# Streaming the weight chunks straight from the input tensors instead of from a contiguous copy in DRAM

## The chip, the cores and the metric

One core of a Trainium2 chip runs the whole kernel. The metric is device time in microseconds (us); medians of several executions are quoted.

## The reference

Two independent parts write the two halves of the output. Part A (a long convolution by Fourier transform) is not touched by the change, except that it shares the DMA engines. Part B is a chain of 64 segments, each a small attention layer that hands 8 memory rows to the next one:

```
for s in range(n_seg):                       # 64 segments of 32 rows
    h = concat(mem, x[32*s : 32*s+32])       # 40 x 1024
    q, k, v = h @ Wq, h @ Wk, h @ Wv         # 1024 x 4096 each
    o = softmax(mask(q k^T * scale)) v       # 32 heads of 128
    o = o @ Wo                               # 4096 x 1024
    mem = o[:8]; out[s] = o[8:]
```

The four matrices are 32 MB in bf16. They do not fit into SBUF, and each segment needs all of them.

## The kernel before

The weights are cut into 64 chunks of 128 x 2048 elements (512 KB, 4 KB per partition). 43 stay in SBUF (`Wearly`, `Wlate`). 21 are streamed; one of these is kept in PSUM, so every segment loads 20: fourteen of the projections (four of Wk, five of Wq, five of Wv) and six of Wo. Loads go to a ring of six tiles, `wring`. A load is issued when the matmuls of an earlier chunk release their ring tile.

```python
W_v = [w.rearrange("(kc p) (g c) -> kc g p c", p=128, g=2) for w in (Wk, Wq, Wv)]
Wo_v = Wo.rearrange("(hp hh e) d -> hp e hh d", hh=2, e=128)
...
def dram_chunk(ch):                 # where the chunk lies in the input tensor
    m, a, g = ch
    return Wo_v[a] if m == 3 else W_v[m][a, g]

def stream_src(ch):                 # where it lies in the copy
    return WS[ring_order.index(ch), :, 0:2048]
...
WS = dram.tile([len(ring_order), 128, PITCH], BF, name="WS")      # PITCH = 2048: contiguous
for ch in ring_order:
    if ch[0] == 3:                  # Wo chunks: DRAM to DRAM, at the start
        nc.gpsimd.dma_start(dst_view(stream_src(ch), ch), dram_chunk(ch))
...
# set-up of part B: the projection chunks pass through SBUF once anyway and are written to WS
nc.sync.dma_start(t[:], dram_chunk(ch))
if ch in streamed:
    nc.gpsimd.dma_start(stream_src(ch), t[:])
...
def fetch():                        # the segment loop
    if loads:
        s, ch = loads.pop(0)
        live[s, ch] = t = ring.tile([128, 2048], BF, tag="wring", name="wring")
        nc.sync.dma_start(t[:], stream_src(ch))
```

So each load reads 512 KB that lie in one piece. In the inputs, a projection chunk is 128 rows of 4 KB that lie 8 KB apart (a row of 4096 elements is shared by two chunks), and a Wo chunk is two runs of 2 KB per partition.

## Time and profile before

| | |
|---|---|
| time | 2419.2 us (2403.4 to 2421.8, 3 runs) |
| set-up (part A, and part B's set-up), until the first `wring` load is issued | 563.8 us |
| segment loop | 1855 us, 28.7 us per segment |

The windows view of the kernel before, over three stretches of the loop; the last columns are the granted TensorE clock, the mean busy share of the 16 DMA engines and the bytes moved per time:

```profile
core 0: us, PE busy (x) PEld busy (x) DVE busy (x) ACT busy (x) POOL busy (x), PEclk, DMA share, GB/s
600.00:1200.00 600.00, 468.98 (x10469) 238.39 (x10468) 164.03 (x615) 142.28 (x273) 87.61 (x294) 0.96 0.99 381
1200.00:1800.00 600.00, 469.17 (x10414) 239.59 (x10418) 163.85 (x614) 141.92 (x272) 87.16 (x293) 0.96 0.98 380
1800.00:2400.00 600.00, 469.26 (x10467) 241.81 (x10460) 164.03 (x614) 142.28 (x273) 86.83 (x292) 0.96 0.98 380
```

The DMA engines are busy 98 to 99% of the time; TensorE is not (469 of 600 us). The chain of waits of the same kernel, by engine and then by line:

```profile
DMA 43%; PE 27%; issue 4%; ACT 1%; DVE 1%; POOL 0%; DVEq 0%; SPq 0%; POOLq 0%; ACTq 0%
DMA wring<-WS 43%; PE acc L708 16%; PE yacc L796 4%; PE tail_acc L657 2%; PE tps L723 1%; PE tps L627 1%; PE S L731 1%; PE S L727 1%; ACT Y L855 1%; PE OTp L769 0%; DVE rec L628 0%; PE S L734 0%; DMA rec<-REC 0%; PE OTp L773 0%; DMA out_dra
```

Waiting for a streamed chunk is the largest part of the chain. The DMA view of the loop (600 to 2400 us): packets of all queues, and the loads with their median time from issue to landing:

```profile
DMA packets 194189, 684.92 MB, mean 381 GB/s; under 512 B 27815, under 2 KB 27815, under 8 KB 193889
...
wring<-WS SPq DMA_DIRECT2D x1255, 512.0 KB, 7.4
```

At 381 GB/s one load of 512 KB takes 1.4 us of the engines, but 7.4 us to land: about five are queued on average. The packet records of the trace show 4096 B packets with a mean of 167 ns.

SyncE's timeline, where the loop's first loads are issued (start, length, instruction):

```profile
563.83 6.58 SPq L597 DMA_DIRECT2D wring<-WS  x6
```

Below is one segment close to the average; the rows are 0–3, 3–8, 8–11, 11–16 and 16–28 us after the segment's start, which here means the ScalarE copy that ends the segment before it (`Y<-yacc`).

```profile
969.59:972.59 3.00, 2.23 (x22) 0.92 (x26) 1.43 (x3) 0.37 (x1) 2.12 (x7) 0.57 1.03 406
972.59:977.59 5.00, 4.84 (x81) 2.05 (x76) 0.42 (x1) 1.17 (x2) 0.00 (x0) 0.92 0.95 308
977.59:980.59 3.00, 1.92 (x32) 0.78 (x28) 0.42 (x1) 0.58 (x1) 0.00 (x0) 1.00 1.00 388
980.59:985.59 5.00, 3.98 (x85) 1.72 (x81) 1.11 (x3) 1.40 (x3) 0.90 (x5) 1.00 1.02 413
985.59:997.59 12.00, 8.78 (x269) 5.06 (x269) 4.31 (x21) 3.51 (x7) 0.57 (x1) 1.00 1.03 406
```

SyncE issues no load for about four us around a segment's start: the tile of a segment's last chunk goes to the chunk that returns from PSUM, so by the code the next load waits until the new segment has used its first streamed chunk (averaged over the segments: the last issue 1.2 us before the start, the next 3.0 us after it). Then six loads follow within 5 us. The rate falls to about 300 GB/s and is back at 413 some ten microseconds later. The engines are also less busy in it: their mean share in the 3–8 us stretch is 0.86 (packet records, 58 segments), though it is 0.98 to 0.99 over the loop.

### The profile page before, as it was taken

The numbers are of one execution on the slowest core, as the hardware profiler recorded it, in microseconds if no ns is written. First come the engines' busy times: TensorE is split into PE (matmuls) and PEld (weight loads), VectorE is DVE, ScalarE is ACT, GpSimd is POOL, SyncE is SP. The second block draws the span as 40 slices with busy tenths as digits, with TensorE's granted clock in tenths as the row PEclk, the third lists the DMA queues.
The fourth block names the chain that finished last, engine by engine and source line by source line (L and its number), as shares of the span: only waits on it lengthen the run. The fifth ranks groups of instructions, "written<-read, shape, count | busy, mean of one in ns | idle before, by whom it ended". The sixth has DMA issues, their size and how long they took to land.

```text
span 2419.0 us, 76567 instructions
## 1 busy us (share of the span) xinstructions
PE 1773.0 (73%) x33620; PEld 883.9 (37%) x33620; DVE 755.4 (31%) x2331; ACT 640.0 (26%) x1143; POOL 365.4 (15%) x1019
## 2 busy tenths in 40 slices
PE   2665369764787777777778778778778777777876
PEld 1221034322343434434343434343434343444433
DVE  5978321111222222222223222222222222222222
ACT  6965011111222222222222222222222222222222
POOL 5034100000111111111111111111111111111111
PEclk9788669887999999999999998999999999999999
DMA  8886974659999999999999999999999999999997
GB/s 290 311 282 206 369 264 114 201 192 389 383 376 396 372 388 378 395 365 375 388 379 399 373 381 370 399 362 379 364 384 384 379 363 382 369 399 375 373 390 284
DMA packets 308487, 842.05 MB, mean 348 GB/s; under 512 B 83676, under 2 KB 91900, under 8 KB 308151
## 3 DMA queue, kind: packets, MB, share of 16 engines
q1 hardware_dynamic: 277992, 767.72, 83.3%
q0 software_dynamic: 20048, 45.76, 5.5%
q10 hardware_dynamic: 10112, 23.68, 2.9%
q8 instruction: 263, 4.31, 0.7%
q14 instruction: 72, 0.59, 0.1%
HBM read 777.66 MB, written 62.39 MB: 347 GB/s over the span
## 4 chain that ended last, share of the span: by engine, by line
DMA 43%; PE 27%; issue 4%; ACT 1%; DVE 1%; POOL 0%; DVEq 0%; SPq 0%; POOLq 0%; ACTq 0%
DMA wring<-WS 43%; PE acc L708 16%; PE yacc L796 4%; PE tail_acc L657 2%; PE tps L723 1%; PE tps L627 1%; PE S L731 1%; PE S L727 1%; ACT Y L855 1%; PE OTp L769 0%; DVE rec L628 0%; PE S L734 0%; DMA rec<-REC 0%; PE OTp L773 0%; DMA out_dram<-Y 0%
## 5 line engine op out<-in xcount | busy, mean ns | idle before, releaser
L708 PEld LDWEIGHTS <-rec 128*32 128x32 bf16 x12288 | 322.2, 98 | 568.2 <-issue 324.5
L708 PE MATMUL acc<-wring,rec 128*32 128x512 bf16 x3840 | 396.6, 396 | 164.0 <-DMA wring<-WS 156.4
L717 ACT CAST qkv_sb<-acc 128x512 bf16<-128x512 f32 x384 | 224.7, 585 | 824.2 <-PE acc L708 824.2
L708 PE MATMUL acc<-Wearly,rec 128*32 128x512 bf16 x4608 | 383.5, 404 | 17.1 <-DVE rec L628 17.0
L708 PE MATMUL acc<-Wlate,rec 128*32 128x512 bf16 x3840 | 332.7, 388 | 0.3 <-issue 0.3
L796 PEld LDWEIGHTS <-OT 128*32 128x32 bf16 x8192 | 221.4, 100 | 259.8 <-issue 191.8
L796 PE MATMUL yacc<-Wlate,OT 128*32 128x256 bf16 x5120 | 239.7, 288 | 41.3 <-issue 41.1
L796 PE MATMUL yacc<-wring,OT 128*32 128x256 bf16 x3072 | 173.8, 288 | 123.3 <-DMA wring<-WS 103.0
L685 POOL COPY KT<-rec 128x128 bf16<-128x128 bf16 x128 | 38.3, 299 | 649.9 <-PE S L734 550.7
L628 DVE COPY rec<-tps 128x64 bf16<-128x64 bf16 x64 | 12.3, 192 | 383.6 <-PE tps L627 378.8
L739 DVE TENSOR_REDUCE mx<-S 128x5 f32<-128x200 f32 x128 | 47.1, 368 | 269.8 <-PE S L734 262.8
L861 POOL DMA_DIRECT2D out_dram<-Y x64 | 45.9, 717 | 517.6 <-ACT Y L855 508.7
L782 ACT CAST OT<-OTp 128x512 bf16<-128x512 f32 x128 | 74.9, 585 | 174.7 <-PE OTp L773 170.1
L855 ACT CAST Y<-yacc 128x256 bf16<-128x256 f32 x64 | 23.8, 372 | 305.1 <-PE yacc L796 305.1
L723 PE MATMUL tps<-ident,qkv_sb 128*128 128x128 bf16 x1024 | 101.9, 222 | 0.0
L621 POOL DMA_DIRECT2D rec<-REC x64 | 37.3, 583 | 405.7 <-issue 199.9
L786 DVE CAST OTB<-OTp 128x128 bf16<-128x128 f32 x128 | 34.7, 271 | 195.1 <-ACT OT L782 195.1
L815 DVE COPY KT<-tps 128x512 bf16<-128x512 bf16 x64 | 27.2, 425 | 216.5 <-PE tps L723 216.5
L723 PEld LDWEIGHTS <-qkv_sb 128*128 128x128 bf16 x1024 | 58.1, 98 | 82.2 <-issue 65.9
L540 PE MATMUL kb_ps<-XBT,Wearly 128*128 128x512 bf16 x288 | 84.2, 383 | 1.2 <-ACT XBT L507 1.2
L692 POOL COPY QBm<-rec 128x32 bf16<-128x32 bf16 x512 | 83.8, 209 | 0.0
L818 DVE COPY QT<-tps 128x512 bf16<-128x512 bf16 x64 | 27.2, 425 | 165.0 <-PE tps L723 165.0
(201 smaller groups left out, 2256.7 us busy)
## 6 DMA issues: line engine op xcount, KB each, us to landing
wring<-WS SPq DMA_DIRECT2D x1281, 512.0 KB, 7.4
rec<-REC POOLq DMA_DIRECT2D x64, 192.0 KB, 6.3
SK<-s_sb SPq DMA_DIRECT2D x16, 512.0 KB, 4.5
SU<-s_sb SPq DMA_DIRECT2D x16, 512.0 KB, 3.9
Kg<-SK ACTq DMA_DIRECT2D x32, 256.0 KB, 4.7
Ug<-SU SPq DMA_DIRECT2D x32, 256.0 KB, 5.3
REC<-stage SPq DMA_DIRECT2D x4, 2048.0 KB, 13.2
pw<-in_B_Wv_dram SPq DMA_DIRECT2D x16, 512.0 KB, 8.4
```

Source lines behind the costliest of these rows:

```text
L540: nc.tensor.matmul(ps[:], lhsT=ws[kc][:, hl * 128:(hl + 1) * 128], rhs=XBT[:, kc].rearrange("p s t -> p (s t)"), start=(kc == 0), stop=(kc ...
L657: nc.tensor.matmul(self.acc[32 * dq:32 * dq + 32, 0:256], lhsT=self.OTB[:, c, 4 * g + i, :], rhs=w[:, o:o + 256], start=first, stop=not se ...
L685: nc.gpsimd.tensor_copy(KT[:, :, :, 32:40], KBs[:, 128 * g:128 * g + 128].rearrange("p (c i t) -> p i c t", c=4, i=4))
L692: nc.gpsimd.tensor_copy(q[:, :, 40 * i:40 * i + 8], QBs[:, 128 * g:128 * g + 128].rearrange("p (c i t) -> p c i t", c=4, i=4)[:, :, i, :])
L708: nc.tensor.matmul(self.acc[32 * c:32 * c + 32, :], lhsT=hT[:, kc, :], rhs=w[:, c * 512:(c + 1) * 512], start=(kc == 0), stop=(kc == 7), t ...
L717: nc.scalar.copy(sb[:], self.acc[:])
L723: nc.tensor.transpose(tp[:, i * 128:(i + 1) * 128], sb[:, i * 128:(i + 1) * 128], ident[:])
L739: nc.vector.tensor_reduce(out=mx[:], in_=S, op=ALU.max, axis=AX.X)
L782: nc.scalar.copy(OT[:], o_view(g)[:, :, :, 0:32])
L796: nc.tensor.matmul(yacc[32 * dq:32 * dq + 32, 0:256], lhsT=OT[:, c, i, :], rhs=w[:, hh * 1024 + dq * 256:hh * 1024 + (dq + 1) * 256], star ...
L855: nc.scalar.copy(Y[:], yacc[:, 0:256])
L861: nc.gpsimd.dma_start(bass.AP(outb.tensor, outb.offset + SEG * s * 2048, [[256, 4], [2048, 32], [1, 256]]), Y[:])
```

## The change

Intent: read the streamed chunks from where they lie, and save the writes of the copy: 15 of 512 KB from SBUF, and six DRAM-to-DRAM copies of 512 KB.

```diff
-PITCH = 2048
@@
-    def stream_src(ch):
-        return WS[ring_order.index(ch), :, 0:2048]
@@
-    WS = dram.tile([len(ring_order), 128, PITCH], BF, name="WS")
-    for ch in ring_order:
-        if ch[0] == 3:
-            nc.gpsimd.dma_start(dst_view(stream_src(ch), ch), dram_chunk(ch))
@@
                     nc.sync.dma_start(t[:], dram_chunk(ch))
-                    if ch in streamed:
-                        nc.gpsimd.dma_start(stream_src(ch), t[:])
@@
-            nc.sync.dma_start(t[:], stream_src(ch))
+            nc.sync.dma_start(dst_view(t[:], ch), dram_chunk(ch))
```

More of the change, by code (lines that the diff above doesn't have):

```diff
@@ L420, in b_kernel @@
     late = resident[NEARLY:]
-    ring_order = [ch for ch in order if ch in streamed]
     def dram_chunk(ch):
```

## The prediction

> **What bounds the kernel now.** The segment loop (from about 575 us, three quarters of the span) is bound by the DMA engines: in the windows view their share is 0.98 to 0.99 in each third of 600–2400 us, PE's 78%. The chain of waits is 43% DMA `wring<-WS`, 27% PE; the DMA view shows 7.4 us for a 512 KB load to land, though the engines need about 1.4 us, so there is always a backlog. Before the loop, 240–336 us is DMA-bound too (share 0.84 to 1.03 in most 10 us windows), 340–430 us PE-bound, and 531–565 us is the DMA-bound load of the resident weights.
>
> **Removed.** 15 writes `WS<-pw` (512 KB each) and 6 DRAM-to-DRAM copies of output-projection chunks.
> - The copies are issued at 23–27 us, under ScalarE's table building (ACT 9.9 of 10 us busy): 0 to 2 us.
> - Nine writes fall into the DMA-bound 240–336 us. One is 128 packets of 4096 B at about 170 ns (packet records), over 16 engines 1.4 us: 12 us together, of which I expect about 8.
> - Six lie under PE work: about 2 us.
>
> Setup: about -10 us (-3 to -17).
>
> **Moved.** The loop loads 20 chunks per segment (one of the 21 stays in PSUM).
> - Fourteen are projection chunks: rows of 4 KB at a pitch of 8 KB instead of contiguous. `Wearly`, `Wlate` and `pw` are read so already: in 300–310 and 548–558 us their packets take 161 to 164 ns, against 167 ns for WS in the loop. I expect no cost.
> - Six are output-projection chunks, now two runs of 2 KB per partition. The resident ones already move as 2048 B packets: 87 to 88 ns mean in 547–562 us, 84 at best. Two take 175 ns where one of 4096 B takes about 164: 9 to 14 ns more per 4 KB. The Trainium skill, "DMA: Bandwidth & Descriptors", section "Why small descriptors are slow (HBM only)", gives a fixed overhead per packet; the trace agrees in sign (2 x 84 against 159 ns).
>
> Per engine: 64 segments x 6 chunks x 8 rows = 3072 pairs x 11 ns = 34 us (27 to 43), nearly all on the critical path.
>
> SyncE's issue grows only from 0.32 us to about 0.37 us per load (`Wlate` from Wo), under 1.4 us, so it does not bind.
>
> **Sum.** 2419 - 10 + 34 = about 2442 us, range 2420 to 2470. Faster by over 2%: 0.02; within 2%: 0.84; slower by over 2%: 0.14. Most likely about 1% slower.
>
> **What would show it.** The loop's period (28.5 us per segment) grows by about 0.5 us. About 49,000 packets of 2048 B in the loop at 87 to 90 ns; 4096 B packets unchanged near 165 ns. DMA share stays 0.98, GB/s falls from 381 to about 374. The first `wring` load is issued about 10 us earlier than at 563.8 us.
>
> **What would make it wrong.**
> - Strided 4 KB reads slower in steady state: 4 ns more per packet over 14 chunks would be 29 us. The same page (entry "HBM row pitch at large powers of two") tells of slow pitches from 512 KiB; 8 KB is far below, and no stretch of this trace shows a loss.
> - 2 KB packets stretched more under full load (95 ns would give 80 us).
> - More packets queued holding up SyncE, so that fewer loads are in flight and engines idle between bursts.
> - A larger gain in setup, if loads there get reordered.

## The result

| | before | after |
|---|---|---|
| median of 4 runs in the same rounds | 2416.6 us | 2497.1 us |
| ratio | | 1.034 (95% interval 1.029 to 1.040) |
| first `wring` load issued (profiled run) | 563.8 us | 555.6 us |
| loop, from there to the end of the span | 1855.2 us | 1940.0 us |

Ratios here and below are the mean time of one kernel's fast runs over that of the other's of the same rounds, so they are not quite the ratio of the quoted medians. The result is outside the predicted range: 80 us slower, not 23. By the 2% rule of the record the whole change, E1 and E5 are slower, E3 is unclear, and E2, E4, E7 and E8 are the same; where an effect under 2% is called real below, its 95% interval leaves out 1.

The windows view after, same stretches as before:

```profile
600.00:1200.00 600.00, 451.54 (x9920) 228.66 (x9922) 155.73 (x584) 134.52 (x258) 84.22 (x280) 0.94 0.98 361
1200.00:1800.00 600.00, 454.65 (x10051) 229.76 (x10044) 156.39 (x585) 136.30 (x262) 84.26 (x280) 0.96 0.99 365
1800.00:2400.00 600.00, 458.80 (x9948) 227.48 (x9950) 155.64 (x584) 135.08 (x259) 83.61 (x277) 0.93 0.99 361
```

The DMA share is unchanged at 0.98 to 0.99, but it moves 361 to 365 GB/s in place of 381. A busy share counts the time that packets take, whether they are quick or slow. The chain of waits after:

```profile
DMA 58%; PE 29%; issue 3%; DVE 3%; POOL 1%; ACT 1%; SPq 0%; ACTq 0%; DVEq 0%; POOLq 0%
DMA wring<-in_B_Wo_dram 20%; DMA wring<-in_B_Wv_dram 18%; PE acc L695 14%; DMA wring<-in_B_Wq_dram 10%; PE kb_ps L527 5%; DMA wring<-in_B_Wk_dram 3%; PE yacc L783 3%; PE tail_acc L644 2%; PE vb_ps L540 2%; DMA X_sb<-in_B_x_dram 1%; PE tps L
```

And the DMA view of the loop after, with one line per source:

```profile
DMA packets 230969, 652.07 MB, mean 362 GB/s; under 512 B 26496, under 2 KB 26496, under 8 KB 230683
...
wring<-in_B_Wo_dram SPq DMA_DIRECT2D x360, 512.0 KB, 7.7
wring<-in_B_Wv_dram SPq DMA_DIRECT2D x297, 512.0 KB, 8.6
wring<-in_B_Wq_dram SPq DMA_DIRECT2D x297, 512.0 KB, 7.5
wring<-in_B_Wk_dram SPq DMA_DIRECT2D x239, 512.0 KB, 7.7
```

Wv loads take 8.6 us to land, Wo 7.7, against 7.4 before. The timeline of SyncE's first loop loads after:

```profile
555.59 4.61 SPq L584 DMA_DIRECT2D wring<-in_B_Wk_dram  x2
```

Set-up is 8.2 us shorter in these two profiled runs, close to the prediction. The loop takes 84.8 us more. The packet records of 600 to 2400 us say how (worked out from all packets of SyncE's queue):

| | before | after |
|---|---|---|
| 2048 B packets, mean | none | 87.4 ns |
| 4096 B packets, median | 161 ns | 159 ns |
| 4096 B packets, mean | 167.0 ns | 176.5 ns |
| 4096 B packets over 200 ns | 2.4% | 7.8% |

The 2 KB packets came out as predicted (87 to 90 ns). The usual 4 KB packet is not slower (159 against 161 ns); there is a tail of long ones. One segment of the kernel after, close to its average, with the same five stretches as above:

```profile
1793.84:1796.84 3.00, 2.23 (x22) 0.90 (x26) 1.42 (x3) 0.37 (x1) 0.75 (x2) 0.56 1.05 416
1796.84:1801.84 5.00, 4.92 (x84) 2.10 (x78) 0.42 (x1) 1.17 (x2) 1.38 (x6) 0.92 0.86 274
1801.84:1804.84 3.00, 1.15 (x20) 0.38 (x15) 0.42 (x1) 0.59 (x1) 0.00 (x0) 0.94 0.96 365
1804.84:1809.84 5.00, 4.83 (x81) 1.79 (x77) 0.74 (x2) 0.62 (x2) 0.90 (x5) 0.70 1.01 356
1809.84:1821.84 12.00, 9.39 (x245) 5.12 (x241) 4.68 (x22) 4.04 (x8) 0.60 (x1) 0.86 1.04 395
```

Averaged over 58 segments, the packets that start in each stretch move, in GB/s:

| us after the segment's start | 0–3 | 3–8 | 8–11 | 11–16 | 16–28 |
|---|---|---|---|---|---|
| before | 373 | 299 | 367 | 407 | 406 |
| after | 382 | 271 | 362 | 359 | 391 |
| 4 KB packets over 200 ns, before | 1.3% | 11.2% | 4.4% | 0.7% | 0.4% |
| the same, after | 1.5% | 16.9% | 6.7% | 12.3% | 2.7% |

The difference in each stretch times its length, divided by about 405 GB/s, is 0.97 us per segment lost between 3 and 16 us, where of the weights only projection chunks move, and 0.44 us between 16 and 28 us, where the 2 KB runs of Wo move. The mean period of a segment grew from 28.73 to 30.10 us.

### The profile page after: what moved, and what is told of

Its sections match the earlier page's. It is cut to its first block, busy times and chain, and to the rows that moved or that the text cites. A ratio compares the mean times of both kernels' runs of the same rounds, so it can differ in the third digit from the quotient of the medians.

```text
span 2495.6 us, 76528 instructions
## 1 busy us (share of the span) xinstructions
PE 1791.2 (72%) x33620; PEld 879.5 (35%) x33620; DVE 754.9 (30%) x2331; ACT 639.9 (26%) x1143; POOL 354.7 (14%) x998
## 4 chain that ended last, share of the span: by engine, by line
DMA 58%; PE 29%; issue 3%; DVE 3%; POOL 1%; ACT 1%; SPq 0%; ACTq 0%; DVEq 0%; POOLq 0%
DMA wring<-in_B_Wo_dram 20%; DMA wring<-in_B_Wv_dram 18%; PE acc L695 14%; DMA wring<-in_B_Wq_dram 10%; PE kb_ps L527 5%; DMA wring<-in_B_Wk_dram 3%; PE yacc L783 3%; PE tail_acc L644 2%; PE vb_ps L540 2%; DMA X_sb<-in_B_x_dram 1%; PE tps L710 1%; DMA pw<-in_B_Wv_dram 1%; POOL Yre L341 1%; DMA Wlate<-in_B_Wo_dram 1%; DMA out_dram<-ot 1%
## 5 line engine op out<-in xcount | busy, mean ns | idle before, releaser
L695 PE MATMUL acc<-wring,rec 128*32 128x512 bf16 x3840 | 407.0, 409 | 215.3 <-DMA wring<-in_B_Wq_dram 126.9
L695 PEld LDWEIGHTS <-rec 128*32 128x32 bf16 x12288 | 327.2, 100 | 634.9 <-issue 370.2
L695 PE MATMUL acc<-Wearly,rec 128*32 128x512 bf16 x4608 | 393.3, 414 | 19.2 <-DVE rec L615 17.2
L695 PE MATMUL acc<-Wlate,rec 128*32 128x512 bf16 x3840 | 342.8, 401 | 0.0
L783 PEld LDWEIGHTS <-OT 128*32 128x32 bf16 x8192 | 214.0, 99 | 273.6 <-issue 240.9
L783 PE MATMUL yacc<-wring,OT 128*32 128x256 bf16 x3072 | 168.1, 284 | 149.2 <-DMA wring<-in_B_Wo_dram 133.8
L783 PE MATMUL yacc<-Wlate,OT 128*32 128x256 bf16 x5120 | 233.4, 284 | 24.4 <-issue 23.8
L615 DVE COPY rec<-tps 128x64 bf16<-128x64 bf16 x64 | 12.3, 192 | 390.3 <-PE tps L614 379.9
L733 DVE TENSOR_REDUCE ssum<-S 128x5 f32<-128x200 f32 x128 | 47.2, 368 | 131.6 <-ACT S L729 131.6
```

Source lines behind the costliest of these rows:

```text
L695: nc.tensor.matmul(self.acc[32 * c:32 * c + 32, :], lhsT=hT[:, kc, :], rhs=w[:, c * 512:(c + 1) * 512], start=(kc == 0), stop=(kc == 7), t ...
L733: nc.vector.tensor_reduce(out=ssum[:], in_=S, op=ALU.add, axis=AX.X)
L783: nc.tensor.matmul(yacc[32 * dq:32 * dq + 32, 0:256], lhsT=OT[:, c, i, :], rhs=w[:, hh * 1024 + dq * 256:hh * 1024 + (dq + 1) * 256], star ...
```

## The experiments

Theory S: the reads at 8 KB pitch cost most, but only for some microseconds after the pause at each segment's start; the 2 KB runs cost the small part that was predicted. Rivals: the 2 KB packets disturb the 4 KB ones (M); the input tensors lie in a slower place of DRAM; strided reads are slower everywhere.

### E1: only Wo keeps its copy

```diff
-                    if ch in streamed:
-                        nc.gpsimd.dma_start(stream_src(ch), t[:])
-            nc.sync.dma_start(t[:], stream_src(ch))
+            nc.sync.dma_start(t[:], stream_src(ch) if ch[0] == 3 else dram_chunk(ch))
```

> The six output-projection chunks keep their contiguous copy (4096 B packets); only the 14 projection chunks are read from the input weights (4 KB rows, 8 KB pitch). Theory S (the strided reads of the projection chunks cost about 1 us per segment through long 4096 B packets, 2 KB packets only 0.42 us): about 2416 + 62 - 8 (setup) = 2470 us (2455 to 2485), share of 4096 B packets over 200 ns about 6 to 8% as in the changed kernel (7.9%) against 2.4% before. Rival M (the 2 KB packets disturb the 4 KB ones, the stride itself is free, as I predicted): 2405 to 2415 us and 2.4% long packets.

Measured: 2476.5 us against 2419.2 us, ratio 1.024 (1.021 to 1.027). 5.8% of the 4 KB packets take over 200 ns, and there is no 2 KB packet in the loop. A row of its windows view, and then 3–8 and 11–16 us of one of its segments:

```profile
1200.00:1800.00 600.00, 458.08 (x10024) 227.41 (x10013) 156.39 (x585) 135.52 (x260) 83.90 (x280) 0.94 0.97 365
2028.75:2033.75 5.00, 5.00 (x85) 2.08 (x76) 0.42 (x1) 1.17 (x2) 0.00 (x0) 0.93 0.76 233
2036.75:2041.75 5.00, 5.00 (x85) 1.86 (x78) 0.74 (x2) 0.97 (x2) 0.90 (x5) 0.70 1.02 365
```

The loss in rate (365 GB/s) is there without any 2 KB packet. Rival M falls. Given to loads in the order of issue (128 packets each, 58 segments), the packets of E1 take 0.88 us per segment and engine more than before, 56 us over 64 segments. Only 0.29 us of it lies in the first four chunks issued after the pause, at about 5–11 us; 0.50 us lies in the five Wv chunks that follow, at about 11–18 us. There are two dips, and the later one is the larger.

### E2: only the projections keep their copy

```diff
-    for ch in ring_order:
-        if ch[0] == 3:
-            nc.gpsimd.dma_start(dst_view(stream_src(ch), ch), dram_chunk(ch))
-            nc.sync.dma_start(t[:], stream_src(ch))
+            nc.sync.dma_start(dst_view(t[:], ch), dram_chunk(ch) if ch[0] == 3 else stream_src(ch))
```

> The projection chunks keep their contiguous copy; only the six output-projection chunks are read directly, as 2 KB runs. Theory S: 2416 + 27 = about 2443 us (2433 to 2452), long 4096 B packets stay near 2.4%. Rival M: most of the 80 us, 2480 to 2500 us, with long packets near 8%.

Measured: 2437.8 us, ratio 1.009 (1.006 to 1.011), about 21 us. Long 4 KB packets: 3.0%. Its windows row:

```profile
1200.00:1800.00 600.00, 465.92 (x10352) 235.81 (x10341) 162.02 (x604) 139.94 (x269) 86.56 (x288) 0.95 1.00 377
```

E1 (+57 us) and E2 (+21 us by the ratio) add up to 78 us; the whole change cost 80 by the medians and 83 by the ratio. Within the noise the two parts add up, and the part that was predicted to be free is the large one.

### E3 and E4: the copy with gaps between its rows

```diff
-PITCH = 2048
+PITCH = 4096      # E3: rows 8 KB apart      (E4: PITCH = 2304, rows 4.5 KB apart)
```

> The kernel before with PITCH 4096: the copy is kept for all 21 chunks, but its 4 KB rows lie 8 KB apart, as in the input weights; no 2 KB packet, same queues. If the pitch is what costs (theory S1): slower than before by at least the 62 us of the projection chunks, 2470 to 2500 us, and long 4096 B packets 7 to 10%. If it is the place of the input tensors in DRAM (rival S2): as before, 2405 to 2425 us.

> The kernel before with PITCH 2304: rows 4.5 KB apart, not a power of two. If the cost comes from rows of several engines falling together at power-of-two distances (theory S1a), as before or some us faster (2395 to 2420 us), with long packets at or under 2.4%. If any gap between the rows costs (rival S1b: only contiguous reads are fast), slower, 2440 us or more.

Measured: E3 2468.0 us, ratio 1.023 (1.017 to 1.029); its four runs scatter from 2461 to 2496 us, and 4.5% of the packets are long. E4 2419.0 us, ratio 1.000 (0.998 to 1.003), 2.5% long. A private copy, read in packets of the same size, is slow at a pitch of 8 KB and not at 4.5 KB. So gaps as such cost nothing, and neither the input tensors nor the 2 KB runs are needed for a loss. E3 came out a little under the range expected of S1 (2470), with fewer long packets than the 7 to 10% expected, and its dip lies in 3–10 us only (252 to 289 GB/s in 4–8 us), while E1 shows a second one at 12 us (342 GB/s).

### E5: the copy laid out like the inputs

```diff
     def stream_src(ch):
+        if ch[0] != 3:
+            return WX_v[ch[0]][ch[1], ch[2]]
...
+    WX = [dram.tile([1024, 4096], BF, name=f"WX{m}") for m in range(3)]
+    WX_v = [w[:].rearrange("(kc p) (g c) -> kc g p c", p=128, g=2) for w in WX]
```

> The copy of the 15 projection chunks is kept, but laid out in DRAM as the inputs are (1024 x 4096 matrices, so also the distances between successive chunks are those of the inputs); output-projection chunks contiguous. If distances between chunks matter besides the pitch, it is E1 plus the setup writes: 2476 + 8 = about 2485 us, with the dip to 342 GB/s that E1 shows 12 us after a segment's start. If the place of the input tensors makes that dip, it is the 8 KB pitch run's time, about 2465 us, with 400 GB/s there.

Measured: 2496.8 us against 2422.9 us, ratio 1.031 (1.027 to 1.035). A segment takes 29.87 us, as in E1 (29.93) and more than in E3 (29.41). So a private copy is as slow per segment as the inputs, if the distances between its chunks are theirs too: the place of the input tensors is not what costs. The shape of the dip was half as expected: 375 to 391 GB/s at 12–16 us, not 342, and a slower recovery before. The time is also above the 2485 us expected. That distances between chunks matter besides the pitch is therefore supported by the period, not explained.

### M1: the loads alone

A kernel of loads only (it writes zeros): 80 loads of 512 KB per stage to a ring of six tiles, which VectorE releases. Its output is wrong, which doesn't matter for the time.

```python
for drain in (True, False):
    for name, cs in tests + tests[:1]:       # contiguous, 8 KB, alternating halves, 4.5 KB, 16 KB, ...
        for i in range(80):
            t = ring.tile([128, 2048], BF, tag="r", name=n)
            if i == 0 or drain and i % 10 == 0:
                nc.vector.memset(t[:, 0:8], 0.0)      # behind the reads of all earlier loads
            nc.sync.dma_start(d, src)
            ...
```

> Only loads of 512 KB (wrong result on purpose, zeros), 80 per stage, six tiles of ring, no compute. Nine stages that drain the queue after every ten loads, then nine that keep it full. Theory L (rows at a power-of-two pitch make the 16 engines collide when they start together after a pause; skew hides it later): in the drained stages 8 KB and 16 KB pitch deliver at least 8% less than contiguous and than 4.5 KB pitch, with long 4096 B packets (over 200 ns) several times as many; in the full stages 8 KB is within 2% of contiguous. Rival A (pitch is slower always): the same loss in both kinds of stage. Rival N (it needs the compute engines' traffic or the other queues): all 4096 B stages within 2%. 2 KB runs: 4 to 6% below contiguous in both kinds.

The windows view of M1 by stage. The first five rows are stages that drain the queue after every ten loads: contiguous, 8 KB, 4.5 KB and 16 KB pitch, and the 2 KB runs of Wo. The last four keep the queue full: contiguous, 8 KB, 4.5 KB, 2 KB runs.

```profile
core 0: us, DVE busy (x) POOL busy (x), PEclk, DMA share, GB/s
1.96:129.58 127.62, 19.61 (x123) 0.00 (x0) 1.00 0.84 329
129.58:269.29 139.71, 19.60 (x123) 0.00 (x0) 1.00 0.83 300
401.12:528.22 127.10, 19.60 (x123) 0.00 (x0) 1.00 0.85 330
528.22:663.77 135.55, 19.61 (x123) 0.00 (x0) 1.00 0.82 310
927.13:1064.21 137.08, 19.60 (x123) 0.00 (x0) 1.00 0.85 306
1192.65:1299.54 106.89, 13.61 (x81) 0.00 (x0) 1.00 0.99 393
1299.54:1407.65 108.11, 13.63 (x81) 0.00 (x0) 1.00 0.99 388
1514.29:1621.53 107.24, 13.63 (x81) 0.00 (x0) 1.00 0.99 391
1943.13:2055.38 112.25, 13.62 (x81) 0.00 (x0) 1.00 1.02 374
```

With the draining, 8 KB moves 300 GB/s against 329 for contiguous rows and 330 for 4.5 KB; 16 KB lies between, at 310. With a full queue the pitches shown are within 1.3% of each other (388 to 393), less than the two contiguous stages of this run differ (393, and 402 when repeated; 329 and 327 with draining). 16 KB missed its expectation: 6% under contiguous, not at least 8%. The stages not shown as rows: the chunks in the loop's own order moved 310 GB/s with draining, and 328 at the same order with contiguous rows. By packet records, 11.2% of the 8 KB stage's packets were long with draining (4.0% contiguous), and 1.7% with a full queue. Microsecond by microsecond after a restart, averaged over the eight restarts, the 8 KB stage moved 232, 269, 244, 264, 324, 355, 359, 393, 414 GB/s from the second microsecond on; contiguous rows had 395 in the third and fell below 380 only once after that (328). So the loss lies in the first eight microseconds, which is why rival A (slower always) falls; rival N falls because there is no compute here. Contiguous rows lose something just after a restart too. The 2 KB runs cost about 5% with a full queue (374 against 393) and 7% with draining (306 against 329), where 4 to 6% was expected.

### M2: where in the run, and how empty the queue must be

```python
six = lambda a, b: [(a if i % 10 < 6 else b)[i % 16] for i in range(80)]
tests = [..., ("mflatfirst", six(F, K), 0), ("mpitchfirst", six(K, F), 0),
         ("mflata", F, 1), ("mpitcha", K, 1), ...]         # F contiguous, K at 8 KB pitch
            consume(i - left if i % 10 == 0 else i - 5)     # wait until `left` loads remain
```

> Loads alone again (wrong result on purpose), every tenth load held until 0, 1, 2 or 3 of the earlier ones are left. If the restart is where the 8 KB pitch costs: contiguous for the first six loads after the drain and 8 KB for the last four runs as contiguous throughout (about 330 GB/s), the other way round as 8 KB throughout (about 302). If a stretch of 8 KB loads costs wherever it stands, both lie half way (about 315). With 1, 2 and 3 loads left the loss of the 8 KB pitch against contiguous shrinks from 8.7% towards the 1.4% of the full queue; if it is gone with one load left, only a fully empty queue matters.

Measured, in GB/s over each stage (packet records, from first issue to last packet):

| loads left at the hold | 0 | 1 | 2 | 3 |
|---|---|---|---|---|
| contiguous | 330 | 347 | 377 | 398 |
| 8 KB pitch | 302 | 325 | 328 | 359 |

8 KB first, contiguous last: 306, as expected of the restart. Contiguous first, 8 KB last: 315, which was not expected: a dip (283 GB/s, 49% long packets in its worst microsecond) came when the strided loads began, ten microseconds after the restart. And the loss did not shrink with the loads left; with three left it is still 10%. So a pause that only thins the queue is enough, and "the first loads after a restart" was too narrow a reading. Two were left: every onset of a strided run costs, or the engines stay in a bad state for some ten microseconds after a hold, whatever they read meanwhile. M3 tests the first.

### E7 and E8: in the real kernel, copy only the chunks after the pause, or all but those

```diff
+    restart = {(0, 5, 1), (1, 0, 1), (1, 3, 1), (1, 6, 1), (2, 1, 0), (2, 4, 0)}
+    copied = {ch for ch in ring_order if ch[0] == 3 or ch in restart}       # E8: ch not in restart
-                    if ch in streamed:
+                    if ch in copied:
-            nc.sync.dma_start(t[:], stream_src(ch))
+            nc.sync.dma_start(t[:], stream_src(ch) if ch in copied else dram_chunk(ch))
```

> In the real kernel: output-projection chunks and the six chunks issued in the first 6 us after the segment's pause are read from the contiguous copy, the other nine projection chunks directly (eight loads per segment). Restart theory: nearly the whole loss of the direct projections (57 us in E1) is gone: 2410 to 2425 us, dip as before. Rival (each direct load costs the same, 57/14 = 4 us per chunk of the loop): 2416 - 4 + 8 x 4.4 = about 2447 us.

> The complement: only the six chunks issued after the pause are read directly, all others from the contiguous copy. Restart theory: most of E1's loss stays, 2455 to 2480 us, dip as deep as in E1. Rival (same cost per load): 2416 - 3 + 6 x 4.4 = about 2439 us.

Measured: E7 2415.6 us, ratio 0.999 (0.996 to 1.002); E8 2456.9 us, ratio 1.016 (1.013 to 1.020), about 40 us. One segment of each, 3–8, 8–11, 11–16 and 16–28 us after its start. E7:

```profile
1089.34:1094.34 5.00, 4.93 (x80) 2.07 (x76) 0.42 (x1) 1.17 (x2) 0.00 (x0) 0.90 0.95 325
1094.34:1097.34 3.00, 1.54 (x28) 0.60 (x21) 0.42 (x1) 0.58 (x1) 0.00 (x0) 1.00 0.97 373
1097.34:1102.34 5.00, 3.83 (x81) 1.53 (x76) 0.74 (x2) 1.33 (x3) 0.89 (x5) 1.00 1.02 412
1102.34:1114.34 12.00, 9.32 (x277) 5.29 (x273) 4.68 (x22) 3.32 (x7) 0.58 (x1) 1.00 1.02 407
```

E8:

```profile
1071.66:1076.66 5.00, 4.86 (x76) 2.00 (x65) 0.42 (x1) 1.17 (x2) 0.00 (x0) 0.92 0.87 263
1076.66:1079.66 3.00, 1.54 (x28) 0.62 (x27) 0.42 (x1) 0.58 (x1) 0.00 (x0) 1.00 0.96 367
1079.66:1084.66 5.00, 4.00 (x85) 1.60 (x78) 0.74 (x2) 1.17 (x3) 0.90 (x5) 1.00 1.01 371
1084.66:1096.66 12.00, 9.09 (x269) 5.35 (x269) 4.68 (x22) 3.48 (x8) 0.59 (x1) 1.00 1.03 412
```

E7 reads eight of the fourteen projection chunks per segment at 8 KB pitch and loses nothing: 325 and 412 GB/s where the kernel before has 308 and 413. E8 reads six and loses most of what E1 loses. At equal cost per load E7 would have been the slower of the two. Among 20 loads, it is the six after the pause that cost. E8 hit the range expected of the restart theory (2455 to 2480 us), not the rival's 2439, and E7's zero refutes the equal cost. But the six chunks always come after the pause, so these runs do not show whether it is their time or their addresses. And E8 has both dips: of its 0.57 us of extra packet time per segment, 0.25 us lies in the first four chunks after the pause and 0.31 us in the Wv chunks, nearly all at about 11–16 us (371 GB/s above).

E7 is also the best version found that needs fewer writes, but it is not shown to be faster than the kernel before, so nothing here beats it.

### M3: onset or time since the hold

```python
for name, n in tests:                       # n = 6, 12, 20, 40, 0, 6
    for rep in range(6):                    # from an empty queue
        for kind, w, count in (("flat", F, n), ("pitch", K, 10)):
            ...                             # n contiguous loads, then ten at 8 KB pitch
```

> Loads alone (wrong result on purpose): from an empty queue n contiguous loads, then ten at 8 KB pitch, n = 0, 6, 12, 20, 40, six times each. After m2 two readings are left. Onset: every beginning of a run at 8 KB pitch costs the same, so the ten pitched loads take as much extra time (about 2 us over 10 x 1.3 us) for every n, and their long packets stay near 10 to 17%. Alignment: the engines are aligned by the drain and drift apart with time, so the loss of the pitched loads shrinks with n and at n = 40 is nearly gone (long packets 1 to 3%); this fits the kernel with the restart chunks copied, where pitched loads that follow twelve contiguous ones show no dip.

The DMA view of M3, the strided loads behind 6, 12, 20, 40, 0 and again 6 contiguous ones, with the median time to landing in the last column:

```profile
msixapitch<-in_B_Wk_dram SPq DMA_DIRECT2D x60, 512.0 KB, 7.9
mtwelvepitch<-in_B_Wk_dram SPq DMA_DIRECT2D x60, 512.0 KB, 7.4
mtwentypitch<-in_B_Wk_dram SPq DMA_DIRECT2D x60, 512.0 KB, 7.4
mfortypitch<-in_B_Wk_dram SPq DMA_DIRECT2D x60, 512.0 KB, 7.4
mnonepitch<-in_B_Wk_dram SPq DMA_DIRECT2D x60, 512.0 KB, 7.4
msixbpitch<-in_B_Wk_dram SPq DMA_DIRECT2D x60, 512.0 KB, 8.0
```

Behind 12 or more the strided loads land in 7.4 us, like contiguous ones; behind six they need 7.9 to 8.0. A median can hide a loss, though: `mnonepitch`, from an empty queue, has 7.4 too and loses most. The packets decide:

| contiguous loads ahead | 0 | 6 | 12 | 20 | 40 | 6 again |
|---|---|---|---|---|---|---|
| long packets of the ten strided loads | 9.4% | 6.1% | 1.2% | 0.3% | 0.2% | 6.3% |
| long packets of the second strided load alone | 46% | 50% | 9% | 0% | 0% | 51% |
| time of the ten | – | 13.44 us | 12.86 us | 12.88 us | 12.81 us | 13.48 us |

The times are from the mean of the 16 completion marks of the load before to that of the tenth strided load (means of six); ten contiguous loads take 12.80 us. From the empty queue the first ten loads take 16.3 us strided, and 14.8 to 15.1 us contiguous in the stages with 12 or more of those. Onset falls: with 20 contiguous loads ahead, beginning a strided run costs nothing, and with 12 nearly nothing. In this kernel of loads alone, somewhere between six and twelve contiguous loads (some 8 to 16 us at 1.3 us each) have to pass after the queue was empty before rows 8 KB apart are free.

The segment loop does not follow this number: in E7 three strided Wv chunks come right behind the six contiguous ones after the pause, yet 0 to 3% of their packets are long. (The last words expected of M3 overlook these three.) The loop's pause does not empty the queue as M3 does, and no run here scales one to the other.

## Why the prediction was wrong

- **What bounds the loop.** Right: the DMA share was 0.98 before and after, and the rate lost per segment (0.97 and 0.44 us above) came back as 1.37 us of period.
- **Set-up, predicted -10 us.** Right in size: the first loop load came 8.2 us earlier in the profiled runs. In the profiles of E2 to E5 the point lies at 565.7 to 571.1 us though, a scatter that no run explains.
- **The 2 KB runs of Wo, predicted +34 us.** Right in kind, and somewhat too large: E2 measured 21 us. The packets took 87.4 ns as predicted; the 4 KB packets that they replaced were 167 ns long on average, not 164, tail included, so a pair costs about 8 ns more in place of 11 (2 x 87.4 - 167 = 7.8 ns, times 3072 pairs = 24 us).
- **The strided projection reads, "I expect no cost".** This is the step that failed. E1 measured +57 us net, so about 65 us with the 8 us of saved set-up added back; by its packet records the reads took 0.88 us more per segment and engine, 56 us in all. The evidence for the step was packets of 161 to 164 ns in two stretches, 300–310 and 548–558 us. Both were long runs with a full queue, at 405 and 402 GB/s, and M1 confirms that there the pitch is nearly free. The loop is another case: a pause at each segment's start, then a burst. The prediction listed "strided 4 KB reads slower in steady state" as a danger. The danger was real, but in M1's full queue it hardly occurred (388 against 393 GB/s).
- **The packets, predicted "unchanged near 165 ns".** Wrong by the tail alone: the median went from 161 to 159 ns, the mean from 167.0 to 176.5. Comparing medians would have hidden all of it.
- **GB/s, predicted 374.** It was 361 to 365.
- **The Trainium skill.** The page "DMA: Bandwidth & Descriptors", section "Latency and other measured facts", entry "HBM row pitch at large powers of two", gives rates of copies at row pitches of 512 KiB (207 GB/s, hardly under the full 214) to 8 MiB (103), and offers, as an inference, that per-partition streams in lock step fall on the same memory channels. It advises padding the pitch or laying tiles out contiguously. The prediction read the smallest listed pitch as a limit under which nothing happens. Here the pattern was seen at 8 and 16 KB (M1 with draining: 300 and 310 GB/s against 329), and padding (E4, ratio 1.000) or a contiguous copy cured it, as the entry says.

What is shown: in the kernel, rows 8 KB apart cost and rows 4.5 KB apart do not (E3, E4), and the cost comes with the six chunks issued after the pause (E7, E8); in loads alone, the same chunks lose after the queue was drained and hardly with a full queue (M1, M3). That the pause makes the loss in the kernel too is argued from these together: no run removed the pause, or put other chunks behind it.

What is open: the later dip, at 11–18 us. It is the larger half of E1's loss (0.50 of 0.88 us), E5 and E8 have it (0.44 and 0.31 us), E3 and E7 do not. In M1, rows 8 KB apart had recovered by the ninth microsecond after a restart (393 GB/s), and E1 is back at 382 GB/s between its dips, so the restart alone does not account for the later one. E3 against E5 suggests that the distances between chunks matter for it. Open, too, is why M2's loss does not shrink with the loads left.

What is only inferred: why the packets are long at all. Engines that start together and read at fixed power-of-two distances may fall on the same part of DRAM until they have drifted apart; no trace here names a DRAM channel, so this is not shown.

## What to carry to other kernels

A transfer's cost taken from one stretch of a trace holds for that state of the queue: look for the same access pattern in the same rhythm of bursts and pauses before calling it free, and look at the mean and the tail of the packets rather than the median. A DMA share near 1 says that the engines are occupied, not that they are quick, so read the GB/s beside it, in slices of one loop period. Where a loop streams weights in bursts, try a contiguous or oddly pitched copy made once: here the copy of the projections cost about 8 us of set-up and saved about 65 us, and copying Wo and the six chunks issued after the pause was enough (E7).

## What the Trainium skill lacked or had wrong

- "DMA: Bandwidth & Descriptors", entry "HBM row pitch at large powers of two": starts at 512 KiB. Loads of 128 rows of 4 KB lose at much smaller pitches in bursts: 300 GB/s at 8 KB and 310 at 16 KB against 329 contiguous (M1, drained every ten loads).
- Same entry: at a pitch of 4 MiB a padding of 4 KiB restores the rate and 192 B does not. For rows of 4 KB, 512 B between them were enough (4.5 KB apart: 330 GB/s in M1, ratio 1.000 in E4).
- Same entry: it does not say that the loss depends on the queue's history. With a full queue 8 KB moved 388 GB/s against 393 contiguous, and behind twelve contiguous loads after an empty queue ten strided ones took 12.86 us, behind six 13.44 us (M3; ten contiguous: 12.80 us).
- Same page, section "Specifications": a minimum transfer for line rate of 512 B. Runs of 2 KB still lost 5% against runs of 4 KB on a full queue (374 against 393 GB/s in M1), and 21 us of the kernel (E2).
